# Channel mixing in six blocks of 512 tokens, some across two batches, in place of eight blocks of 384

## The chip, the cores and the metric

The kernel runs on one core of one Trainium2 chip. The metric is the device time of one execution in microseconds (us), and the median over the runs is compared. The core has a matrix engine (PE, with its weight loads listed apart as PEld), a vector engine (DVE), a scalar engine (ACT), GpSimd (POOL) and a queue engine (SP) that issues most of the transfers. Matmul results land in PSUM, in which this kernel keeps eight buffers, called banks here: four under the tag `sc` (among them `po`), three under `sh` (`ph`, `yp`) and one under `xT`.

## What is computed

A decayed causal attention over 4 batches, 8 heads, 768 tokens and head size 64 gives `x` of shape (4, 768, 512). A mixer follows: first over the tokens of each batch, then over the channels of each token.

```python
def _moe_ref(x, w_tok1, w_tok2, w_ch1, w_ch2):
    xt = x.transpose(0, 2, 1)
    h = np.maximum(xt @ w_tok1, 0.0) @ w_tok2
    u = x + h.transpose(0, 2, 1)
    h2 = np.maximum(u @ w_ch1, 0.0) @ w_ch2
    return (u + h2).astype(np.float32)
```

The change concerns the last three lines, the channel mixing: `u` is 4 x 768 = 3072 tokens of 512 channels, `w_ch1` is 512 x 1536 and `w_ch2` is 1536 x 512. Each token is independent of the others there, so the 3072 tokens can be cut into blocks anywhere.

## The kernel before

The activations lie in SBUF transposed, with the channels on the partitions: `uT[b]` is a tile of 128 partitions x 4 channel groups x 768 tokens for each batch `b`. Attention writes it (L299), the token mixing adds to it (L441), the channel mixing reads it and adds to it again (L629).

To keep float32 accuracy, each operand of a mixing matmul is split into a high and a low part in a 32-bit matmul type, and each product is three matmuls: high x high, low x high, high x low. The token mixing does that at L416 (256 columns) and L436 (384 columns).

The channel mixing takes the tokens in eight blocks (b, sh), half a batch of `SB` = 384 tokens each, and the 1536 hidden channels in six groups of 256 (`NG` = 6, two tiles of 128, `jj`, in each). A unit is one pair (group g, block k); the 48 units go group by group. In a unit:

- `mm1(g, k, jj)` for the two `jj`: 12 matmuls of 128 x 384 into one PSUM bank `ph` (4 channel groups x 3 products, L605), then ACT makes the high part of the ReLU, `hh` (L609), and DVE the low part, `hl` (L610).
- `mm2` of the unit before, one for each of the four output channel groups t: 6 matmuls into a bank `po` (L626) and one DVE addition into `uT` (L629). So each unit has 24 matmuls of `mm1` and 24 of `mm2`, all of 384 columns; mm1 of this unit and mm2 of the one before alternate: mm1, two mm2, mm1, two mm2.

The high and low parts of a block's tokens, `uh` and `ul`, are made once by `split_block`: four steps, each an ACT cast (L500) and a POOL subtraction (L501). Blocks 0 and 1 are split during attention, put on a list of small steps, `waiting`, that is worked off between the other instructions; the others are split in the units of the first group, one block ahead.

The weights of a group arrive as 64-bit words by DMA and are narrowed in four pieces by a chain of one ACT, five DVE, one ACT and one POOL instruction of 512 elements (L342 to L360). Each piece is loaded in one unit of the group before and worked off through `waiting` in the next.

The last ten pieces of the token mixing (the list `groups`, of which attention takes 38 of 48) are spread over the first units by `rest`: two in unit 0, four in unit 1, four in unit 2. In the last group the finished blocks 0 to 6 are turned by DVE (L636) into a buffer `y`, of which there are two, and written to memory by 16 DMAs per block from SP (L641). The last block is turned by PE (L650) into bank `yp`, copied by ACT (L654) into `ylast`, and written by three DMAs (L658): one for t = 0 and 1 from ACT, one for t = 2 from SP, one for t = 3 from ACT.

The order of all engines is the order in which the code is written (a manual schedule); each engine runs its instructions in that order, except that PE's weight loads run ahead.

Of the kernel before, what the change touches and what calls it, by code (L numbers as in the profile page):

```python
# [9 lines left out]
F32 = mybir.dt.float32  # L10
F32R = mybir.dt.float32r
# [10 lines left out]
def kernel(  # L22
# [35 lines left out]


    ET = mybir.EngineType  # L60
# [2 lines left out]
    waiting = deque()  # L63
# [5 lines left out]


    upool = ctx.enter_context(tc.tile_pool(name="upool", bufs=1))
    uT = [upool.tile([P, NP, S], F32, name=f"uT{b}") for b in range(B)]
    ident = upool.tile([P, P], F32, name="ident")
    wa = ctx.enter_context(tc.tile_pool(name="wa", bufs=1))
    up = ctx.enter_context(tc.tile_pool(name="up", bufs=1))
# [3 lines left out]
    def bank(tag, nm, n):  # L79
        return ps.tile([P, n], F32, tag=tag, bufs={"sc": 4, "xT": 1, "sh": 3}[tag], name=nm)  # L80
# [82 lines left out]
    n = 1  # L163
# [282 lines left out]
    NG = NJ // JG  # L446
# [38 lines left out]
        return w[:, i * 1024 : (i + 1) * 1024], w[:, 2048:2560], w[:, 2560:3072]  # L485


    blocks = [(b, sh) for b in range(B) for sh in range(2)]
    uhl = {}

    def split_block(k, pool):

        b, sh = blocks[k]
        ub = uT[b][:, :, sh * SB : (sh + 1) * SB]
        uh = pool.tile([P, 4, SB], F32R, name=f"uh{k}")
        ul = pool.tile([P, 4, SB], F32R, name=f"ul{k}")
        uhl[k] = uh, ul

        def step(t):
            nc.scalar.copy(out=uh[:, t], in_=ub[:, t])  # L500
            nc.gpsimd.tensor_sub(out=ul[:, t], in0=ub[:, t], in1=uh[:, t].bitcast(F32))  # L501

        return [lambda t=t: step(t) for t in range(4)]

# [17 lines left out]
    for i in range(-2, NI):  # L522
        if 0 <= i + 1 < NI:
            scores(i + 1)
            scale_q(i + 1)
        if i >= 0:
            outputs(i, 0)
        place = state(i + 1) if 0 <= i + 1 < NI else None
        if i >= 0:
            outputs(i, 1)  # L530
        if i + 2 < NI:
            turn_q(i + 2)
        work = [groups.popleft() for _ in range(take.get(i, 0))]
# [24 lines left out]
        if i + 4 < NI:  # L558
            load_kq(i + 4)
        if i == -1:  # L560
            load_w1()
        if i == 1:
            load_w2()
        if 0 <= i < 3:
            convert_w1(i)
        if 2 <= i < 4:
            convert_w2(i - 2)
        if i == 3:
            convert_w2(2)
        if i == 5:  # L570
            weights[0], load, convert = load_group(0, wa, early_scratch)
        if 5 <= i < 9:
            load(i - 5)
        if 6 <= i < 10:
            convert(i - 6)
        if i == 9:
            waiting.extend(split_block(0, up))
        if i == 11:
            waiting.extend(split_block(1, up))
    later(99)  # L580
    att.close()
    wp = ctx.enter_context(tc.tile_pool(name="wp", bufs=1, reuse_waits="tile"))
# [2 lines left out]
    cp = None  # L585
# [10 lines left out]
    def mm1(g, k, jj):  # L596
        uh, ul = uhl[k]
        c1h, c1l, _, _ = weights[g]
        js = slice(jj * P, (jj + 1) * P)
        nm = f"{g}{k}{jj}"  # L600
        ph = bank("sh", f"ph2{nm}", SB)
        i = 0
        for ct in range(4):
            for w, x in ((c1h, uh), (c1l, uh), (c1h, ul)):
                nc.tensor.matmul(out=ph, lhsT=w[:, ct, js], rhs=x[:, ct], start=(i == 0), stop=(i == 11))  # L605
                i += 1
        hh = hp.tile([P, SB], F32R, tag="hh2", name=f"hh2{nm}")
        hl = hp.tile([P, SB], F32R, tag="hl2", name=f"hl2{nm}")
        nc.scalar.activation(hh, ph, AF.Relu)  # L609
        nc.vector.scalar_tensor_tensor(  # L610
            out=hl, in0=ph, scalar=0.0, in1=hh.bitcast(F32), op0=ALU.max, op1=ALU.subtract
        )
        hs[g, k, jj] = (hh, hl)

    ys = {}

    def mm2(g, k, t):
        b, sh = blocks[k]
        _, _, c2h, c2l = weights[g]
        po = bank("sc", f"po{g}{k}{t}", SB)  # L620
        cs = slice(t * P, (t + 1) * P)
        i = 0
        for jj in range(JG):
            hh, hl = hs[g, k, jj]
            for w, h in ((c2h, hh), (c2l, hh), (c2h, hl)):
                nc.tensor.matmul(out=po, lhsT=w[:, jj, cs], rhs=h, start=(i == 0), stop=(i == 3 * JG - 1))  # L626
                i += 1
        ub = uT[b][:, t, sh * SB : (sh + 1) * SB]
        nc.vector.tensor_add(out=ub, in0=po, in1=ub)  # L629
        if g < NG - 1 or k == len(blocks) - 1:  # L630
            return

        if t == 0:
            ys[k] = cp.tile([P, SB // 32, 4, 32], F32, tag="y", bufs=2, name=f"y{k}")
        y = ys[k]
        nc.vector.transpose(out=y[:, :, t, :], in_=ub)  # L636
        if t % 2 == 1:
            to = out[b, sh * SB : (sh + 1) * SB].rearrange("(blk s) (t q c) -> q s blk t c", s=32, t=4, q=4)
            for n in range(4):
                for tt in (t - 1, t):  # L640
                    nc.sync.dma_start(out=to[n, :, :, tt], in_=y[n * 32 : (n + 1) * 32, :, tt])  # L641

    def finish(t, ylast):

        k = len(blocks) - 1
        b, sh = blocks[k]
        yp = bank("sh", f"yp{t}", SB)
        for c in range(SB // P):
            cs = slice(c * P, (c + 1) * P)
            nc.tensor.transpose(  # L650
                out=yp[:, cs], in_=uT[b][:, t, sh * SB + c * P : sh * SB + (c + 1) * P], identity=ident
            )
        es = slice(t * P, (t + 1) * P)
        nc.scalar.copy(out=ylast[:, :, es], in_=yp.rearrange("p (c e) -> p c e", e=P))  # L654
        to = out[b, sh * SB : (sh + 1) * SB].rearrange("(c s) e -> s c e", s=P)
        if t > 0:
            es = slice(0 if t == 1 else t * P, (t + 1) * P)
            (nc.sync if t == 2 else nc.scalar).dma_start(out=to[:, :, es], in_=ylast[:, :, es])  # L658

    units = [(g, k) for g in range(NG) for k in range(len(blocks))]  # L660
    rest = [[], [], []]
    for n, g in enumerate(groups):
        rest[0 if n < 2 else 1 + (n - 2) // 4].append(g)
    splits = deque()
    for i, (g, k) in enumerate(units):
        if i == 3:
            p1.close()
            cp = ctx.enter_context(tc.tile_pool(name="cp", bufs=1, side="right", reuse_waits="tile"))
        if g == 0 and 2 <= k + 1 < len(blocks):
            splits.extend(split_block(k + 1, uq if k < 3 else cp))  # L670
        first = 1 if g == 0 else 0
        if g + 1 < NG:
            if k == first:
                weights[g + 1], load, convert = load_group(g + 1, wa if g % 2 else wp, scratch)
            if first <= k < first + 4:
                load(k - first)
            if first < k < first + 5:
                convert(k - first - 1)
        for x in range(2):
            for jj in range(x * JG // 2, (x + 1) * JG // 2):  # L680
                mm1(g, k, jj)
                later(2)
            for _ in range(4):
                if splits:
                    splits.popleft()()
            for t in (2 * x, 2 * x + 1):
                if i < len(rest) and t < len(rest[i]):
                    rest[i][t]()
                if i >= 1:
                    mm2(*units[i - 1], t)  # L690
                    later(1)
    ylast = cp.tile([P, SB // P, DM], F32, name="ylast")
    for t in range(4):
        mm2(*units[-1], t)
        if t >= 2:
# [30 lines left out]
```

## Time and profile before

| What | Value |
|---|---|
| device time, median of 3 runs | 612.38 us (612.28 to 614.78) |
| span of the profiled execution, first to last instruction | 1471.3 us |
| PE busy in it | 1461.3 us of the span, 4426 matmuls |
| channel mixing, matmuls | 1152 at L605 and 1152 at L626, 384 columns each |
| first matmul after the start of the span | 5.65 us |
| last matmul of the channel mixing to the end of the span | 6.8 us |
| DVE, ACT, POOL busy in it | 343.6, 154.9, 159.2 us |

The profiled execution is a different one from the timed runs, and it is 2.4 times as long as their median; no device time beside its span is recorded for it. Matmuls overlap in the trace (one starts before the listed end of the one before), so what a matmul costs is read from the distance of starts, or from the chain of work that ended last, and not from the mean duration of one. A row of a group of instructions reads: line, engine, operation, output<-inputs, shape, count | busy us, mean ns of one | idle us of the engine just before them and who ended the idle time.

### The profile page before, as it was taken

To read this page: it belongs to the slowest core of one execution; us is meant where nothing else is said; L and a number is where in the kernel's file an instruction comes from. 1 tells how busy PE (TensorE), PEld (TensorE's weight loads), DVE (VectorE), ACT (ScalarE), POOL (GpSimd) and SP (SyncE) were. 2 spreads that over 40 slices of the span, in tenths; PEclk is the share of its full clock that TensorE was granted. 3 is DMA by queue.
4 is the path that set the end of the run, shared out by engine and by line. 5 is a ranking of instruction groups with operands and counts; after the bars stand their busy time and mean duration, and the time that the engine had idled before them with its cause. 6 is when DMAs were issued, how large, how long until landed. Compare 5 with 4: busy or idle time off the path is not lost.

```text
span 1471.3 us, 10762 instructions
## 1 busy us (share of the span) xinstructions
PE 1461.3 (99%) x4426; PEld 1160.3 (79%) x4426; DVE 343.6 (23%) x654; ACT 154.9 (11%) x315; POOL 159.2 (11%) x155
## 2 busy tenths in 40 slices
PE   8999999999999999999999999999999999999998
PEld 6788788798887777777777777777777777777776
DVE  3333233312111222122211221122211222112222
ACT  2221111110110111000000110010000000000000
POOL 5242212231011121000000000000000000000000
DMA  9423331210000010001000000000000000002222
GB/s 193 108 44 68 71 69 33 43 33 15 15 1 14 15 29 0 0 29 29 0 1 14 29 14 0 0 24 20 15 0 0 29 0 0 0 11 40 36 35 51
DMA packets 144498, 41.61 MB, mean 28 GB/s; under 512 B 137664, under 2 KB 138816, under 8 KB 144448
## 3 DMA queue, kind: packets, MB, share of 16 engines
q1 hardware_dynamic: 143504, 40.32, 13.2%
q8 instruction: 35, 0.57, 0.2%
q10 hardware_dynamic: 944, 0.59, 0.1%
q14 instruction: 15, 0.12, 0.0%
HBM read 34.61 MB, written 6.29 MB: 28 GB/s over the span
## 4 chain that ended last, share of the span: by engine, by line
PE 99%; DMA 0%; ACT 0%; SPq 0%; issue 0%
PE po L626 35%; PE ph L605 35%; PE ph L416 6%; PE pu L436 6%; PE sc L258 4%; PE xT L282 4%; PE xT L292 3%; PE kt L183 2%; PE xp L314 2%; PE kv L225 2%; PE qt L200 1%; DMA kn<-in_k_dram 0%; PE yp L650 0%; ACT uT L299 0%; ACT ylast L654 0%; SPq L100 0%
## 5 line engine op out<-in xcount | busy, mean ns | idle before, releaser
L605 PE MATMUL ph<-uh,c1h 128*128 128x384 f32 x384 | 261.2, 680 | 0.0
L605 PE MATMUL ph<-uh,c1l 128*128 128x384 f32 x384 | 261.1, 680 | 0.0
L626 PE MATMUL po<-hl,c2h 128*128 128x384 f32 x384 | 260.9, 679 | 0.0
L626 PE MATMUL po<-hh,c2h 128*128 128x384 f32 x384 | 260.6, 679 | 0.0
L605 PE MATMUL ph<-ul,c1h 128*128 128x384 f32 x384 | 260.5, 678 | 0.0
L626 PE MATMUL po<-hh,c2l 128*128 128x384 f32 x384 | 260.4, 678 | 0.0
L610 DVE SCALAR_TENSOR_TENSOR hl<-ph,hh 128x384 fp32r<-128x384 f32 x96 | 53.5, 557 | 657.9 <-ACT hh L609 617.6
L605 PEld LDWEIGHTS ph<-uh,c1l 128*128 128x128 f32 x384 | 136.1, 354 | 36.4 <-issue 32.3
L605 PEld LDWEIGHTS ph<-uh,c1h 128*128 128x128 f32 x384 | 135.3, 352 | 37.1 <-issue 33.2
L626 PEld LDWEIGHTS po<-hh,c2l 128*128 128x128 f32 x384 | 134.8, 351 | 37.5 <-issue 33.6
L626 PEld LDWEIGHTS po<-hh,c2h 128*128 128x128 f32 x384 | 134.8, 351 | 37.3 <-issue 29.0
L626 PEld LDWEIGHTS po<-hl,c2h 128*128 128x128 f32 x384 | 134.7, 351 | 37.3 <-issue 31.4
L605 PEld LDWEIGHTS ph<-ul,c1h 128*128 128x128 f32 x384 | 135.2, 352 | 36.4 <-issue 32.4
L609 ACT ACTIVATE hh<-ph 128x384 fp32r<-128x384 f32 x96 | 47.1, 491 | 923.8 <-PE po L626 648.7
L629 DVE TENSOR_TENSOR uT<-po,uT 128x384 f32<-128x384 f32 x192 | 104.5, 553 | 165.1 <-PE po L626 163.5
L282 PE MATMUL xT<-a,vn 128*64 128x128 f32 x384 | 75.0, 515 | 0.6 <-ACT uT L299 0.6
L343 POOL TENSOR_TENSOR c1l<-wa,c1h 128x512 fp32r<-128x512 f32 x10 | 12.7, 1272 | 509.0 <-ACT c1h L342 509.0
L292 PE MATMUL xT<-qs,stb 128*64 128x128 f32 x320 | 67.8, 541 | 0.0
L258 PEld LDWEIGHTS sc<-qT,kT 64*128 64x128 f32 x384 | 55.3, 425 | 8.6 <-issue 7.6
L258 PE MATMUL sc<-qT,kT 64*128 64x128 f32 x384 | 61.9, 535 | 0.0
L416 PE MATMUL ph<-xhi,w1h 128*128 128x256 f32 x96 | 53.9, 561 | 0.0
L416 PE MATMUL ph<-xhi,w1l 128*128 128x256 f32 x96 | 50.9, 530 | 0.0
(77 smaller groups left out, 1091.6 us busy)
## 6 DMA issues: line engine op xcount, KB each, us to landing
raw<-in_moe_w_ch_dram SPq DMA_DIRECT2D x20, 512.0 KB, 3.6
kn<-in_k_dram SPq DMA_DIRECT2D x32, 192.0 KB, 3.3
vn<-in_v_dram SPq DMA_DIRECT2D x16, 384.0 KB, 3.6
out_dram<-y SPq DMA_DIRECT2D x112, 48.0 KB, 1.8
qn<-in_q_dram SPq DMA_DIRECT2D x44, 96.0 KB, 3.6
uT<-in_moe_w_tok_dram SPq DMA_DIRECT2D x2, 1536.0 KB, 8.0
uT<-in_moe_w_ch_dram SPq DMA_DIRECT2D x4, 512.0 KB, 3.9
qn<-in_q_dram SPq DMA_DIRECT2D x10, 192.0 KB, 4.5
```

Source lines behind the costliest of these rows:

```text
L183: nc.tensor.transpose(out=kt[:, c * P : (c + 1) * P], in_=kn[:, 3 * g + c].rearrange("p h d -> p (h d)"), identity=ident,)
L225: nc.tensor.matmul(out=to[h * D : (h + 1) * D, c, :], lhsT=kds[i][:, h, c, :], rhs=vns[i][:, h, c, :], start=(c == 0), stop=(c == NC - 2),)
L258: nc.tensor.matmul(out=sc[h][:, c * P : (c + 1) * P], lhsT=kTs[i][r, cs], rhs=qTs[i][r, cs], start=True, stop=True,)
L282: nc.tensor.matmul(out=xT[h * D : (h + 1) * D, cs], lhsT=vns[i][:, h, c, :], rhs=weights_of[i, g, h][:, cg, :], start=(cg == 0), stop=False,)
L292: nc.tensor.matmul(out=xT[h * D : (h + 1) * D, cs], lhsT=st[:, c - 1, h, :], rhs=qss[i][:, c - 1, :], start=False, stop=(cg == 2),)
L416: nc.tensor.matmul(out=ph, lhsT=w[:, c, fs], rhs=x[:, c], start=(i == 0), stop=(i == 3 * NC - 1))
L436: nc.tensor.matmul(out=pu, lhsT=h[:, kk, cs], rhs=w[:, kk, ss], start=(i == 0), stop=(i == 3 * NK - 1))
L605: nc.tensor.matmul(out=ph, lhsT=w[:, ct, js], rhs=x[:, ct], start=(i == 0), stop=(i == 11))
L609: nc.scalar.activation(hh, ph, AF.Relu)
L610: nc.vector.scalar_tensor_tensor(out=hl, in0=ph, scalar=0.0, in1=hh.bitcast(F32), op0=ALU.max, op1=ALU.subtract)
L626: nc.tensor.matmul(out=po, lhsT=w[:, jj, cs], rhs=h, start=(i == 0), stop=(i == 3 * JG - 1))
L629: nc.vector.tensor_add(out=ub, in0=po, in1=ub)
```

## The change

The channel mixing takes the 3072 tokens in `NB` = 6 blocks of `CB` = 512. 512 is two thirds of 768, so of three blocks two lie in one batch each and the middle one takes the last third of one batch and the first third of the next. To address both with one pattern, the four tiles `uT[b]` become one tile `U` of 128 x 48 x 256: batch, channel group and third of the batch in the middle dimension. `block(k, t)` gives the two thirds of block k for channel group t, as a 128 x 2 x 256 pattern.

```diff
+    CB = 512
+    NB = B * S // CB
-    uT = [upool.tile([P, NP, S], F32, name=f"uT{b}") for b in range(B)]
+    U = upool.tile([P, B * NP * 3, S // 3], F32, name="uT")
+    uT = [U[:, b * NP * 3 : (b + 1) * NP * 3].rearrange("p (t c) s -> p t (c s)", t=NP) for b in range(B)]
...
-    blocks = [(b, sh) for b in range(B) for sh in range(2)]
+    def block(k, t):
+        (b, c), (b1, c1) = divmod(2 * k, 3), divmod(2 * k + 1, 3)
+        i, j = 3 * (b * NP + t) + c, 3 * (b1 * NP + t) + c1
+        return U[:, i : j + 1 : j - i]
+    def two(x):
+        return x.rearrange("p (n s) -> p n s", n=2)
...
-            nc.scalar.copy(out=uh[:, t], in_=ub[:, t])
-            nc.gpsimd.tensor_sub(out=ul[:, t], in0=ub[:, t], in1=uh[:, t].bitcast(F32))
+            ub = block(k, t)
+            nc.scalar.copy(out=two(uh[:, t]), in_=ub)
+            nc.gpsimd.tensor_sub(out=two(ul[:, t]), in0=ub, in1=two(uh[:, t]).bitcast(F32))
...
-        if i == 11:
-            waiting.extend(split_block(1, up))
...
-        ph = bank("sh", f"ph2{nm}", SB)
+        ph = bank("sh", f"ph2{nm}", CB)
...
-        po = bank("sc", f"po{g}{k}{t}", SB)
+        po = bank("sc", f"po{g}{k}{t}", CB)
...
-        ub = uT[b][:, t, sh * SB : (sh + 1) * SB]
-        nc.vector.tensor_add(out=ub, in0=po, in1=ub)
+        ub = block(k, t)
+        nc.vector.tensor_add(out=ub, in0=two(po), in1=ub)
...
-    rest = [[], [], []]
+    rest = [[[], [], [], []] for _ in range(2)]
     for n, g in enumerate(groups):
-        rest[0 if n < 2 else 1 + (n - 2) // 4].append(g)
+        i, t = (0, n) if n < 4 else (1, (n - 4) * 2 // 3)
+        rest[i][t].append(g)
...
-        if i == 3:
+        if i == 2:
             p1.close()
...
-        if g == 0 and 2 <= k + 1 < len(blocks):
-            splits.extend(split_block(k + 1, uq if k < 3 else cp))
+        if g == 0 and k + 1 < NB:
+            splits.extend(split_block(k + 1, uq if k < 2 else cp))
...
-    ylast = cp.tile([P, SB // P, DM], F32, name="ylast")
+    ylast = cp.tile([P, CB // 32, 4, 32], F32, tag="y", bufs=2, name="ylast")
+    ylast = ylast.rearrange("p a b c -> p (a b c)").rearrange("p (c e) -> p c e", e=DM)
```

The buffers `uh`, `ul`, `hh`, `hl`, `y` and `ylast` grow with the block, `ylast` now takes one of the two `y` buffers, the writes to memory follow the new blocks, and in a unit the pieces of `rest` now come after `mm2` and not before it. There are 36 units in place of 48, and 1728 matmuls of 512 columns in place of 2304 of 384 in the channel mixing.

The first place is PE where unit 0 ends and unit 1 begins (names end in group, block and `jj`: `ph2001` is group 0, block 0, second `jj`; `ph2010` is block 1; `pu` is token mixing). Before:

```order
L605 MATMUL ph2001_2523<-uh0_1667,c1l0_1038 128x384
L605 MATMUL ph2001_2523<-ul0_1668,c1h0_1037 128x384
L605 MATMUL ph2010_2550<-uh1_1981,c1h0_1037 128x384
L605 MATMUL ph2010_2550<-uh1_1981,c1l0_1038 128x384
L605 MATMUL ph2010_2550<-ul1_1982,c1h0_1037 128x384
```

And in the changed kernel:

```order
L439 MATMUL pu310_2545<-w2h_124,hl3_2360 128x384
L439 MATMUL pu310_2545<-w2l_125,hh3_2359 128x384
L613 MATMUL ph2010_2563<-uh1_2451,c1h0_1034 128x512
L613 MATMUL ph2010_2563<-uh1_2451,c1l0_1035 128x512
L613 MATMUL ph2010_2563<-ul1_2452,c1h0_1034 128x512
```

Two pieces of the token mixing (`pu300` and `pu310`, twelve matmuls) now stand between the second mm1 of unit 0 and the first mm1 of unit 1; the matmuls themselves are 512 wide.

The second place is ACT from the last attention cast into unit 1 (`uh1` and `uh2` are the high parts of blocks 1 and 2, `hh3` belongs to the token mixing of batch 3, `hh2...` to the channel mixing). Before:

```order
L420 ACTIVATE hh3_2372<-ph301_2433 128x256
L609 ACTIVATE hh2000_2477<-ph2000_2464 128x384
L420 ACTIVATE hh3_2372<-ph310_2481 128x256
L420 ACTIVATE hh3_2372<-ph311_2502 128x256
L609 ACTIVATE hh2001_2536<-ph2001_2523 128x384
L609 ACTIVATE hh2010_2563<-ph2010_2550 128x384
L500 CAST uh2_2540<-uT1_61 128x384 x4
```

And in the changed kernel:

```order
L423 ACTIVATE hh3_2359<-ph301_2420 128x256
L617 ACTIVATE hh2000_2466<-ph2000_2453 128x512
L510 CAST uh1_2451<-uT_60 128x512 x4
L423 ACTIVATE hh3_2359<-ph310_2478 128x256
L423 ACTIVATE hh3_2359<-ph311_2499 128x256
L617 ACTIVATE hh2001_2533<-ph2001_2520 128x512
L617 ACTIVATE hh2010_2576<-ph2010_2563 128x512
L510 CAST uh2_2553<-uT_60 128x512 x4
```

The four casts of block 1 have left the attention loop and stand in unit 0 behind its first ReLU; POOL's four subtractions for `ul1` moved with them.

The third place is the end of PE's work (`po573` and `po553` are the last output group of the last unit, `yp` the turned last block). Before:

```order
L626 MATMUL po573_6207<-hh2571_6147,c2l5_4925 128x384
L626 MATMUL po573_6207<-hl2571_6148,c2h5_4924 128x384
L650 MATMUL yp1_6215<-ident_64,uT3_63 128x128 x3
L650 MATMUL yp2_6221<-ident_64,uT3_63 128x128 x3
L650 MATMUL yp3_6227<-ident_64,uT3_63 128x128 x3
```

And in the changed kernel:

```order
L634 MATMUL po553_5351<-hh2551_5290,c2l5_4374 128x512
L634 MATMUL po553_5351<-hl2551_5291,c2h5_4373 128x512
L657 MATMUL yp1_5359<-ident_61,uT_60 128x128 x4
L657 MATMUL yp2_5366<-ident_61,uT_60 128x128 x4
L657 MATMUL yp3_5373<-ident_61,uT_60 128x128 x4
```

Twelve turns in place of nine stand behind the last matmul of the channel mixing.

More of the change, by code (lines that the diff above doesn't have):

```diff
@@ L485, in early_scratch @@
         return w[:, i * 1024 : (i + 1) * 1024], w[:, 2048:2560], w[:, 2560:3072]
-    blocks = [(b, sh) for b in range(B) for sh in range(2)]
+    def block(k, t):
[4 more added lines that the diff above has]
+        return x.rearrange("p (n s) -> p n s", n=2)
     uhl = {}
     def split_block(k, pool):
[L493 to L496, printed above, removed]
+        uh = pool.tile([P, 4, CB], F32R, name=f"uh{k}")
+        ul = pool.tile([P, 4, CB], F32R, name=f"ul{k}")
         uhl[k] = uh, ul
         def step(t):
-            nc.scalar.copy(out=uh[:, t], in_=ub[:, t])
-            nc.gpsimd.tensor_sub(out=ul[:, t], in0=ub[:, t], in1=uh[:, t].bitcast(F32))
+            ub = block(k, t)
+            nc.scalar.copy(out=two(uh[:, t]), in_=ub)
+            nc.gpsimd.tensor_sub(out=two(ul[:, t]), in0=ub, in1=two(uh[:, t]).bitcast(F32))
         return [lambda t=t: step(t) for t in range(4)]
@@ L606, in mm1 @@
                 i += 1
-        hh = hp.tile([P, SB], F32R, tag="hh2", name=f"hh2{nm}")
-        hl = hp.tile([P, SB], F32R, tag="hl2", name=f"hl2{nm}")
+        hh = hp.tile([P, CB], F32R, tag="hh2", name=f"hh2{nm}")
+        hl = hp.tile([P, CB], F32R, tag="hl2", name=f"hl2{nm}")
         nc.scalar.activation(hh, ph, AF.Relu)
@@ L615 @@
     ys = {}
+    rows = out.rearrange("b s e -> (b s) e")
     def mm2(g, k, t):
-        b, sh = blocks[k]
         _, _, c2h, c2l = weights[g]
-        po = bank("sc", f"po{g}{k}{t}", SB)
+        po = bank("sc", f"po{g}{k}{t}", CB)
         cs = slice(t * P, (t + 1) * P)
@@ L627, in mm2 @@
                 i += 1
-        ub = uT[b][:, t, sh * SB : (sh + 1) * SB]
-        nc.vector.tensor_add(out=ub, in0=po, in1=ub)
-        if g < NG - 1 or k == len(blocks) - 1:
+        ub = block(k, t)
+        nc.vector.tensor_add(out=ub, in0=two(po), in1=ub)
+        if g < NG - 1 or k == NB - 1:
             return
         if t == 0:
-            ys[k] = cp.tile([P, SB // 32, 4, 32], F32, tag="y", bufs=2, name=f"y{k}")
+            ys[k] = cp.tile([P, CB // 32, 4, 32], F32, tag="y", bufs=2, name=f"y{k}")
         y = ys[k]
@@ L637, in mm2 @@
         if t % 2 == 1:
-            to = out[b, sh * SB : (sh + 1) * SB].rearrange("(blk s) (t q c) -> q s blk t c", s=32, t=4, q=4)
+            to = rows[k * CB : (k + 1) * CB].rearrange("(blk s) (t q c) -> q s blk t c", s=32, t=4, q=4)
             for n in range(4):
@@ L643, in finish @@
     def finish(t, ylast):
[L645 to L648, printed above, removed]
+        k = NB - 1
+        yp = bank("sh", f"yp{t}", CB)
+        for c in range(CB // P):
             cs = slice(c * P, (c + 1) * P)
-            nc.tensor.transpose(
-                out=yp[:, cs], in_=uT[b][:, t, sh * SB + c * P : sh * SB + (c + 1) * P], identity=ident
-            )
+            nc.tensor.transpose(out=yp[:, cs], in_=uT[B - 1][:, t, S - CB + c * P : S - CB + (c + 1) * P], identity=ident)
         es = slice(t * P, (t + 1) * P)
         nc.scalar.copy(out=ylast[:, :, es], in_=yp.rearrange("p (c e) -> p c e", e=P))
-        to = out[b, sh * SB : (sh + 1) * SB].rearrange("(c s) e -> s c e", s=P)
+        to = rows[k * CB : (k + 1) * CB].rearrange("(c s) e -> s c e", s=P)
         if t > 0:
@@ L658, in finish @@
             (nc.sync if t == 2 else nc.scalar).dma_start(out=to[:, :, es], in_=ylast[:, :, es])
-    units = [(g, k) for g in range(NG) for k in range(len(blocks))]
-    rest = [[], [], []]
+    units = [(g, k) for g in range(NG) for k in range(NB)]
+    rest = [[[], [], [], []] for _ in range(2)]
     for n, g in enumerate(groups):
-        rest[0 if n < 2 else 1 + (n - 2) // 4].append(g)
+        i, t = (0, n) if n < 4 else (1, (n - 4) * 2 // 3)
+        rest[i][t].append(g)
     splits = deque()
     for i, (g, k) in enumerate(units):
-        if i == 3:
+        if i == 2:
             p1.close()
             cp = ctx.enter_context(tc.tile_pool(name="cp", bufs=1, side="right", reuse_waits="tile"))
-        if g == 0 and 2 <= k + 1 < len(blocks):
-            splits.extend(split_block(k + 1, uq if k < 3 else cp))
+        if g == 0 and k + 1 < NB:
+            splits.extend(split_block(k + 1, uq if k < 2 else cp))
         first = 1 if g == 0 else 0
@@ L691 @@
                     later(1)
-    ylast = cp.tile([P, SB // P, DM], F32, name="ylast")
+                if i < len(rest):
+                    for f in rest[i][t]:
+                        f()
+    ylast = cp.tile([P, CB // 32, 4, 32], F32, tag="y", bufs=2, name="ylast")
+    ylast = ylast.rearrange("p a b c -> p (a b c)").rearrange("p (c e) -> p c e", e=DM)
     for t in range(4):
```

2 lines of the change are left out of this document (removed).

## The prediction

> **What bounds the kernel now.** I read the clock first, then the page's head, then the chain of work that ended last, then PE's waits.
>
> ```profile
> core 0: 1471.3 us, clock 1.000
> span 1471.3 us, 10762 instructions
> PE 1461.3 (99%) x4426; PEld 1160.3 (79%) x4426; DVE 343.6 (23%) x654; ACT 154.9 (11%) x315; POOL 159.2 (11%) x155
> by line: PE po L626 35.0%; PE ph L605 35.0%; PE ph L416 5.8%; PE pu L436 5.8%; PE sc L258 4.1%; PE xT L282 4.0%; PE xT L292 3.2%; PE kt L183 2.0%; PE xp L314 1.9%; PE kv L225 1.6%; PE qt L200 0.6%; DMA kn<-in_k_dram 0.3%; PE yp L650 0.2%; A
> PE kt L183 <- DMA kn<-in_k_dram: 5.6, 1, 5.6
> PE xT L282 <- ACT uT L299: 0.6, 1, 0.6
> ```
>
> PE is the bound: the chain runs through PE from the first transfer to the end, and PE waits 5.6 us for that transfer, 0.6 us once more, and never again. 70% of the chain is the 2304 matmuls that the change rewrites.
>
> The profiled execution is 2.4 times as long as the median, 612.38 us. With PE busy throughout in the profile, the timed runs can only be shorter if PE itself runs faster there. So durations of PE rows must be scaled; those of ACT, DVE, POOL and DMA I take as they stand. Taking away the first wait (5.65 us) and the end behind the last channel matmul (6.8 us, rows below), the pace is (612.38 - 12.45) / (1471.3 - 12.45) = 0.411.
>
> **Fewer, wider matmuls.** Columns stay the same: 2304 x 384 = 1728 x 512 = 884,736. So only what a matmul costs beside its columns can be saved. The chain prices two widths. At 384 columns: 70.0% of 1471.3 us is 1029.9 us, over 2304 matmuls 447.0 ns each. At 256 columns (L416, 288 matmuls): 5.8% is 85.3 us, 296.3 ns each. That is 1.164 and 1.157 ns per column. A line through both has a constant of 3 x 296.3 - 2 x 447.0 = -5 ns; a share is rounded to 0.05%, 0.74 us, which moves 296.3 by 2.6 ns and the constant to anything from -14 to +4 ns. So the row says: proportional to the columns, and a constant of at most 4 ns. Scaled, 512 columns cost 447.0 x 4/3 x 0.411 = 245 ns against 184 ns now.
>
> 576 matmuls fewer save 576 x 4 ns = 2.3 us at the top and cost 576 x 14 ns x 0.411 = 3.3 us at the bottom. I take 2.4 ns, **-1.4 us**: an instruction less is no loss by itself, so the upper half is nearer.
>
> A rule of the Trainium skill ("TensorE: Matmul & The Clock Gate", section "Back-to-back issue gap") gives another size: for streams of weight load and matmul it states a sustained 81 ns at 128 columns and 131 ns at 512. A line through these has a constant of 64 ns, and by it the change would save 576 x 64 ns, 37 us. At 256 and 384 columns it would make 97 to 114 ns, a ratio of 1.17; the chain's ratio here is 447.0 / 296.3 = 1.51, so the trace disagrees.
>
> **What waits on the wider tiles.** ACT and DVE work per matmul result grows with the width, PE's time for it too:
>
> ```profile
> L610 DVE SCALAR_TENSOR_TENSOR hl<-ph,hh 128x384 fp32r<-128x384 f32 x96 | 53.5, 557 | 657.9 <-ACT hh L609 617.6 <-PE po L626 40.3
> L609 ACT ACTIVATE hh<-ph 128x384 fp32r<-128x384 f32 x96 | 47.1, 491 | 923.8 <-PE po L626 648.7 <-PE ph L605 275.0
> L421 DVE SCALAR_TENSOR_TENSOR hl<-ph,hh 128x256 fp32r<-128x256 f32 x16 | 6.8, 424 | 85.5 <-ACT hh L420 85.5
> L420 ACT ACTIVATE hh<-ph 128x256 fp32r<-128x256 f32 x16 | 6.1, 383 | 74.4 <-PE ph L416 74.4
> L351 DVE SCALAR_TENSOR_TENSOR ws<-raw,ws 128x512 uint32<-128x512 uint32 x20 | 14.2, 711 | 0.0
> L360 DVE SCALAR_TENSOR_TENSOR wa<-wa,ws 128x512 uint32<-128x512 uint32 x20 | 13.8, 692 | 0.7
> L354 DVE TENSOR_SCALAR wa<-wa 128x512 f32<-128x512 f32 x20 | 8.3, 417 | 0.0
> ```
>
> 128 more columns add 133 ns on DVE and 108 ns on ACT. The tightest use is the last `hl` of a unit: between the mm1 that makes it and the mm2 that reads it PE has 24 other matmuls. Before that is 24 x 184 ns = 4.4 us at the timed pace, against 0.49 + 0.56 us plus a whole narrowing that DVE may have ahead of it (0.71 + 0.69 + three like L354, 0.42 us each = 2.7): 3.7 us. After: 5.9 us against 0.60 + 0.69 + 2.7 = 4.0 us. Covered before, more so after; nothing.
>
> **The split of block 1, moved into unit 0.** Its casts and subtractions now stand behind ACT's first ReLU. Rows of 512 columns on the same engines:
>
> ```profile
> L342 ACT CAST c1h<-wa 128x512 fp32r<-128x512 f32 x10 | 6.2, 620 | 16.9 <-DVE wa L360 16.9
> L343 POOL TENSOR_TENSOR c1l<-wa,c1h 128x512 fp32r<-128x512 f32 x10 | 12.7, 1272 | 509.0 <-ACT c1h L342 509.0
> ```
>
> From the end of unit 0's first mm1: 0.60 (ReLU) + 0.62 + 1.27 = 2.5 us to the first `ul1`, 2.5 + 3 x 1.27 = 6.3 us to the last. PE has until then two pieces of 18 matmuls of 256 columns (36 x 296.3 x 0.411 = 4.4 us), 12 of 512 (2.9 us) and the two moved pieces of the token mixing (12 x 184 ns = 2.2 us): 9.5 us. Covered by 3 us; nothing. The token mixing pieces keep their matmuls and only change places. The weights' narrowing has four units of a group of six; a unit is a third longer, so it is looser, too. One tile `U` for four adds no wait where the blocks don't overlap.
>
> **The writes of the last group.** SP issues 16 DMAs per block:
>
> ```profile
> L641 SPq DMA_DIRECT2D out_dram<-y x112: 315/467/1763, 1312.4 to 1457.8; - x112
> out_dram<-y SPq DMA_DIRECT2D x112, 48.0 KB, 1.8
> out_dram<-ylast ACTq DMA_DIRECT2D x1, 384.0 KB, 2.7
> out_dram<-ylast SPq DMA_DIRECT2D x1, 192.0 KB, 2.4
> out_dram<-ylast ACTq DMA_DIRECT2D x1, 192.0 KB, 2.1
> ```
>
> 16 x 0.467 = 7.5 us for a block whose unit takes PE 48 x 184 ns = 8.8 us at the timed pace: 85% full, so SP keeps up, but barely. If the mixing's share of the timed run is a tenth smaller, SP falls behind by some tenths of a us per block over seven blocks, and the DMA of t = 2 at the end comes up to about 1 us late. After: 80 issues, 7.5 us in 11.8 us, never behind, provided that an issue of 64 KB costs as one of 48 KB. Between 0 and -1 us: **-0.5 us**.
>
> **The end.** Behind the last channel matmul:
>
> ```profile
> 1464.09 0.72 PE L626 MATMUL po<-hl,c2h 128*128 128x384 f32 x1
> 1464.52 3.01 PE L650 MATMUL yp<-ident,uT 128*128 128x128 f32 x9
> 1464.85 0.56 DVE L629 TENSOR_TENSOR uT<-po,uT 128x384 f32<-128x384 f32 x1 [3.03 <-PE po L626]
> 1465.71 0.48 ACT L654 COPY ylast<-yp 128x384 f32<-128x384 f32 x1 [3.11 <-PE yp L650]
> 1467.57 0.48 ACT L654 COPY ylast<-yp 128x384 f32<-128x384 f32 x1 [0.43 <-PE yp L650]
> 1468.08 0.38 ACTq L658 DMA_DIRECT2D out_dram<-ylast  x1
> ```
>
> Twelve turns for nine: three more of 3.01 / 9 = 0.33 us, 1.0 us at the profile's pace, 0.41 us scaled. The last addition 0.13 us more, the last copy 0.11 us, the last DMA 256 KB for 192: from 2.1 or 2.4 us at 192 KB to 2.7 at 384, some 0.15 us. Sum 0.8 us, between 0.4 (turns hidden behind ACT) and 1.4 (turns at the profile's pace): **+0.8 us**.
>
> **Sum.** 612.38 - 1.4 - 0.5 + 0.8 = 611.3 us, 0.2% less. About 0.5%, 3.1 us, is what a measurement of this kernel can tell from no change, so I call this the same. In the profile, at its own pace, the sum is 1471.3 - 1.4 + 1.4: a span within 10 us of before.
>
> **Rivals.**
>
> *A constant that only the fast pace shows* (faster). Each matmul has one weight load of 128 columns, the same for 384 as for 512. At the profile's pace the loader has time:
>
> ```profile
> 901.44 0.24 PEld L626 LDWEIGHTS po<-hl,c2h 128*128 128x128 f32 x1 [0.18 <-issue]
> 901.87 0.45 PEld L626 LDWEIGHTS po<-hh,c2h 128*128 128x128 f32 x1 [0.19 <-ACT hh L609]
> ```
>
> 0.24 us, with 0.18 and 0.19 us idle before and after it. If loads, unlike matmuls, don't get faster by the whole 2.4, some ns per matmul may stick out at 184 ns. They can't be long: 0.24 us x 2304 = 553 us would leave 59 us for the rest, 30% of the chain. With 6 to 10 ns each the change saves 3.5 to 5.8 us: 609.2 to 606.9 with the end's +0.8 and the writes' -0.5. For it: nothing in the profile excludes it. Against: the chain at two widths has no such constant. 0.24.
>
> *A large constant* (faster). If a third of the 184 ns, 61 ns, were constant, 576 x 61 ns = 35.1 us would go: 577.5 us. Against: 256 columns would then cost 143 ns, 78% of 184, and the chain has 66%. 0.02. The figures of the Trainium skill quoted above come to nearly this.
>
> *Waits before the change that only the fast pace shows* (faster). The `hl` margin above is 0.7 us before and 1.9 after. Were PE late by 0.2 us in the 20 units with a narrowing, 4 us go: 607.3 us. 0.06.
>
> *PE takes steps in width* (slower). Starts of neighbours:
>
> ```profile
> 415.68 0.54 PE L416 MATMUL ph<-xlo,w1h 128*128 128x256 f32 x1
> 415.92 0.53 PE L416 MATMUL ph<-xhi,w1h 128*128 128x256 f32 x1
> 419.08 0.72 PE L605 MATMUL ph<-uh,c1l 128*128 128x384 f32 x1
> 419.51 0.72 PE L605 MATMUL ph<-ul,c1h 128*128 128x384 f32 x1
> ```
>
> 0.24 us at 256 columns, 0.43 at 384: undisturbed neighbours rise by 0.19 for 128 columns, more than in proportion. At that slope 512 columns take 0.62 us where 0.596 would be even: 1728 x 0.62 = 1071 us in place of 2304 x 0.433 = 998, 7% more. Scaled by 0.411: +30 us, 642 us. It decides as soon as the distance at 512 columns is over 4/3 of that at 384. Against: the means, which make the span, are in proportion. 0.06.
>
> *The split of block 1 comes late* (slower). If POOL or ACT is held up for over 3 us around unit 0, unit 1 waits once; all of its 5.1 us of subtractions exposed give 616.4 us. 0.05.
>
> **Chances.** The forecast, 0.57; faster by 0.24 + 0.02 + 0.06; slower 0.06 + 0.05. A little of the first rival's low end falls within 0.5%: faster 0.31, same 0.58, slower 0.11. The range goes from the first rival's far end with the writes' whole term, 606 us, to the bottom of the matmul term and the largest end, 612.38 + 3.3 + 1.4 = 617, cut to 616 since both ends at once are unlikely; it leaves out 577.5, 642 and part of the late split.
>
> **What would show it.** Right: the share of PE in the chain stays at 99%, both changed matmul lines have 1728 matmuls whose distance of starts averages 4/3 of 447 ns, PE's waits stay at the first transfer, and the end behind the last channel matmul grows from 6.8 us to about 8. Wrong: PE waiting in the first two units for `ul1`, a mean distance clearly off 596 ns, or a timed gain over 3 us with nothing waiting, which would make the constant of a matmul larger than 4 ns.

## The result, and the profile after

| | before | after |
|---|---|---|
| device time, median of four runs each | 613.58 us (612.28 to 614.94) | 604.81 us (600.82 to 606.61) |
| ratio, with 95% interval | | 0.9862 (0.9815 to 0.9908) |
| the same in another session (`after_again`) | 610.78 us | 603.14 us, ratio 0.9877 (0.9843 to 0.9911) |

The change makes the kernel faster by 7.6 to 8.8 us, 1.2 to 1.4%. The prediction said 611.3 us, no change, with a range down to 606: it was wrong, on the low side of its range.

The profile of before that the prediction quotes (1471.3 us) is 2.4 times as long as the timed runs, so the comparison below is with a second profile of the same kernel at the timed pace (`before_again`: span 610.7 us, device time of that execution 612.49). The profiled execution of after took 604.87 us, its span is 603.1 us. The granted clock is 0.993 in both.

The page of `before_again` has a row of the granted clock in 40 slices:

```profile
PEclk9989999999999999999999999999999999999998
```

The page of the 1471.3 us profile has no such row, and its trace holds no record of the clock. The 1.000 that the prediction quotes is what the view prints where nothing is recorded, not a measured clock.

The page of after, parts of its head, chain and main groups:

```profile
span 603.1 us, 9441 instructions
PE 581.8 (96%) x3854; PEld 493.9 (82%) x3854; DVE 327.0 (54%) x574; ACT 147.0 (24%) x283; POOL 162.0 (27%) x147
PE 89%; DVE 5%; DMA 2%; ACT 2%; issue 1%; SPq 0%; DVEq 0%; ACTq 0%
L618 DVE SCALAR_TENSOR_TENSOR hl<-ph,hh 128x512 fp32r<-128x512 f32 x72 | 49.8, 692 | 189.5 <-ACT hh L617 189.5
L617 ACT ACTIVATE hh<-ph 128x512 fp32r<-128x512 f32 x72 | 43.1, 599 | 288.8 <-PE po L634 221.4
```

PE is still the bound, but at the timed pace it is 89% of the chain (87% in `before_again`) and not 99%. Most of PE's waits lie in attention:

```profile
PE xT L285 <- ACT uT L302: 6.3, 4, 3.1
PE kt L186 <- DMA kn<-in_k_dram: 5.6, 1, 5.6
PE kv L228 <- POOL kd L210: 1.8, 2, 1.2
PE pu L439 <- DVE hl L618: 0.5, 1, 0.5
```

`before_again` has nearly the same first three, and then:

```profile
PE ph L605 <- DVE hl L610: 1.0, 2, 0.5
```

So in the mixing PE waits 1.0 us before and 0.5 us after. That half microsecond is a small part of the gain; the rest must be read from the matmuls themselves. A stretch of 280 us inside the mixing, in which PE does nothing but channel-mixing matmuls, as a row of the view by windows (from:to, length, PE busy and how many instructions, clock, DMA share, GB/s). `before_again`:

```profile
260.00:540.00 280.00, 280.00 (x1604) 1.00 0.09 27
```

And after:

```profile
260.00:540.00 280.00, 280.00 (x1223) 1.00 0.08 27
```

The row counts every matmul that reaches into the window, also those cut by its edges. So the distance from start to start is taken from the first and the last matmul counted. `before_again`:

```profile
259.83 0.34 PE L626 MATMUL po<-hh,c2h 128*128 128x384 f32 x1
539.84 0.33 PE L605 MATMUL ph<-uh,c1l 128*128 128x384 f32 x1
```

And after:

```profile
259.62 0.39 PE L613 MATMUL ph<-uh,c1h 128*128 128x512 f32 x1
539.80 0.39 PE L634 MATMUL po<-hh,c2l 128*128 128x512 f32 x1
```

That is 280.01 us / 1603 = 174.7 ns from start to start at 384 columns and 280.18 / 1222 = 229.3 ns at 512. In proportion to the columns 512 would take 232.9. The 3.6 ns that each wider matmul is under proportion make the first part of the gain: 2304 x 174.7 = 402.5 us, 1728 x 229.3 = 396.2 us, **6.3 us less**. First and last start of `mm1` and `mm2`, before:

```profile
L605 PE MATMUL ph<-uh,c1h x384: 334/337/443, 184.2 to 594.2; 128*128 128x384 f32 x192
L626 PE MATMUL po<-hl,c2h x384: 334/334/340, 196.2 to 601.4; 128*128 128x384 f32 x192
```

And after:

```profile
L613 PE MATMUL ph<-uh,c1h x288: 387/392/459, 185.2 to 586.6; 128*128 128x512 f32 x144
L634 PE MATMUL po<-hl,c2h x288: 387/389/397, 200.4 to 595.7; 128*128 128x512 f32 x144
```

From the first `mm1` to the last `mm2` it takes 601.4 - 184.2 = 417.2 us before, 595.7 - 185.2 = 410.5 after: 6.7 us less. This counts the waits too; the half microsecond that PE waits less is the likely rest.

The second part is the end. Before, from the last channel matmul:

```profile
601.37 0.34 PE L626 MATMUL po<-hl,c2h 128*128 128x384 f32 x1
601.55 1.42 PE L650 MATMUL yp<-ident,uT 128*128 128x128 f32 x9
603.24 0.40 ACTq L658 DMA_DIRECT2D out_dram<-ylast  x1
603.67 0.86 ACT L654 COPY ylast<-yp 128x384 f32<-128x384 f32 x2 [1.12 <-DMA out_dram<-y]
605.63 0.38 ACTq L658 DMA_DIRECT2D out_dram<-ylast  x1
606.95 0.58 SPq L658 DMA_DIRECT2D out_dram<-ylast  x1
```

And after:

```profile
595.70 0.40 PE L634 MATMUL po<-hl,c2h 128*128 128x512 f32 x1
595.93 1.67 PE L657 MATMUL yp<-ident,uT 128*128 128x128 f32 x12
597.19 0.40 ACTq L663 DMA_DIRECT2D out_dram<-ylast  x1
598.24 0.39 SPq L663 DMA_DIRECT2D out_dram<-ylast  x1
598.73 0.38 ACTq L663 DMA_DIRECT2D out_dram<-ylast  x1
```

The last DMA is issued 5.6 us after the last channel matmul before, and by SP, which was not free earlier; 3.0 us after it now, and by ACT. To the end of the span it takes 610.7 - 601.4 = 9.3 us before and 603.1 - 595.7 = 7.4 after, **1.9 us less**, although the tail itself has more to do. The third part is no effect of the change: the mixing starts at 184.2 us in the one execution and 185.2 in the other. In attention the granted clock falls for a few microseconds in some executions and not in others. The stretch from 30 to 50 us, with the clock as the third number from the right, in `before_again` and in after:

```profile
30.00:50.00 20.00, 15.36 (x210) 0.91 1.10 231
30.00:50.00 20.00, 15.42 (x195) 0.83 1.05 225
```

In `order_384`, `writes_act_384`, `loads_64` and `writes_half_512` the clock is 1.00 in this stretch and the mixing starts at 181.2 to 182.3 us; in `writes_half_384`, with 384 columns, it is 0.83 and the mixing starts at 185.0. So the start goes with the clock and not with the width. -6.7 - 1.9 + 1.0 = -7.6 us, the difference of the spans.

### The profile page after: what moved, and what is told of

Read it like the earlier page. It is cut to its first block, busy times and chain, and to the rows that moved or that the text cites. A ratio compares the mean times of both kernels' runs of the same rounds, so it can differ in the third digit from the quotient of the medians.

```text
span 603.1 us, 9441 instructions
## 1 busy us (share of the span) xinstructions
PE 581.8 (96%) x3854; PEld 493.9 (82%) x3854; DVE 327.0 (54%) x574; ACT 147.0 (24%) x283; POOL 162.0 (27%) x147
## 4 chain that ended last, share of the span: by engine, by line
PE 89%; DVE 5%; DMA 2%; ACT 2%; issue 1%; SPq 0%; DVEq 0%; ACTq 0%
PE ph L613 33%; PE po L634 33%; PE ph L419 6%; PE pu L439 5%; PE xT L285 3%; PE sc L261 3%; PE xT L295 2%; DMA uT<-in_moe_w_tok_dram 2%; PE kt L186 2%; PE kv L228 1%; PE xp L317 1%; DVE uT L354 1%; DMA qn<-in_q_dram 1%; DVE xlo L326 1%; DVE a L270 1%
## 5 line engine op out<-in xcount | busy, mean ns | idle before, releaser
L613 PE MATMUL ph<-ul,c1h 128*128 128x512 f32 x288 | 113.4, 394 | 0.0
L613 PE MATMUL ph<-uh,c1l 128*128 128x512 f32 x288 | 113.2, 393 | 0.0
L613 PE MATMUL ph<-uh,c1h 128*128 128x512 f32 x288 | 113.1, 393 | 0.0
L634 PE MATMUL po<-hh,c2l 128*128 128x512 f32 x288 | 112.8, 392 | 0.0
L634 PE MATMUL po<-hh,c2h 128*128 128x512 f32 x288 | 112.8, 392 | 0.0
L634 PE MATMUL po<-hl,c2h 128*128 128x512 f32 x288 | 112.0, 389 | 0.0
L637 DVE TENSOR_TENSOR uT<-po,uT 128x512 f32<-128x512 f32 x144 | 95.7, 683 | 8.3 <-PE po L634 8.0
L613 PEld LDWEIGHTS ph<-ul,c1h 128*128 128x128 f32 x288 | 54.1, 188 | 12.3
L613 PEld LDWEIGHTS ph<-uh,c1h 128*128 128x128 f32 x288 | 54.2, 188 | 12.1
L613 PEld LDWEIGHTS ph<-uh,c1l 128*128 128x128 f32 x288 | 54.0, 188 | 11.9
```

Of the source, the lines that this page charges most:

```text
L637: nc.vector.tensor_add(out=ub, in0=two(po), in1=ub)
```

## The experiments

Theory 1: a matmul has a constant that doesn't depend on its columns, and fewer matmuls save it. Theory 2: waits before the change that the change removes, by its order or its looser timing. Theory 3: SP's writes of `y` are late before, and hold up the end. All ratios are to the kernel before, on the same chip in the same session.

### The kernel before again

No edit. It gives a profile at the timed pace and the noise.

> The kernel before, unchanged, for a profile at the pace of the timed runs. Theory 1 (a constant per matmul): in the profile of the changed kernel neighbouring matmuls start 120 ns apart at 256 columns, 173 at 384 (token mixing) and 227 at 512, which is columns / 2.4 + 13 ns; so the channel mixing of before starts its matmuls 173 ns apart too, the two lines together take about 2304 x 0.175 = 403 us of the chain against 396 after, and PE waits no more in the channel mixing than after. Theory 2 (waits): the distance of starts is proportional to the columns or less, 170 ns, and PE shows waits for hl, hh or the weights of several us in the channel mixing. Theory 3 (the end): the span behind the last channel matmul is 2 us or more longer than the 7 us after, because the writes from SP come late. Time: 612 to 614 us by all.

610.65 us, ratio 0.9986 (0.9959 to 1.0013). Its rows stand above. In the 1471.3 us profile that the prediction quotes, a stretch of `mm1` and `mm2` alone reads:

```profile
600.00:1300.00 700.00, 700.00 (x1569) 1.00 0.04 11
```

700 us / 1569 = 446 ns (447 without the edges), where the other execution has 174.7 ns. The 1.00 in this row is no reading, as said above, so a lower clock of PE is not excluded; nor is it shown. ACT's ReLU at L609 takes 491 ns in the one and 492 in the other, so ACT kept its pace. Whatever slowed PE also hid the constant; how it did so stays open.

### Every channel matmul cut in two

The changed kernel, with each matmul of 512 columns done as two of 256, one half of the bank after the other: 3456 matmuls for 1728, everything else the same.

```diff
-        for ct in range(4):
-            for w, x in ((c1h, uh), (c1l, uh), (c1h, ul)):
-                nc.tensor.matmul(out=ph, lhsT=w[:, ct, js], rhs=x[:, ct], start=(i == 0), stop=(i == 11))
+        for n in range(2):
+            ns = slice(n * 256, (n + 1) * 256)
+            i = 0
...
+                    nc.tensor.matmul(
+                        out=ph[:, ns], lhsT=w[:, ct, js], rhs=x[:, ct, ns], start=(i == 0), stop=(i == 11)
+                    )
```

(and the same in `mm2`)

> The changed kernel with each matmul of the channel mixing cut into two of 256 columns, 3456 in place of 1728, same columns, same blocks, same other engines. Theory 1 (a constant of 13 ns per matmul): 1728 x 13 = 22.5 us slower than the changed kernel, about 627 us, starts 120 ns apart. Theory 2 or 3 (waits or the end): the number of matmuls matters by 4 ns each at most, up to 7 us slower, 605 to 612 us.

624.16 us, ratio 1.0205 (1.0171 to 1.0238), some 20 us above the changed kernel. The same window of its trace:

```profile
260.00:540.00 280.00, 280.00 (x2337) 1.00 0.09 28
```

Its first and last matmul counted:

```profile
259.77 0.28 PE L640 MATMUL po<-hh,c2l 128*128 128x256 f32 x1
539.92 0.28 PE L615 MATMUL ph<-uh,c1h 128*128 128x256 f32 x1
```

280.15 us / 2336 = 119.9 ns at 256 columns. A line through 256 and 512 has 0.427 ns per column and a constant of 2 x 119.93 - 229.28 = 10.6 ns; it gives 174.6 ns at 384, where 174.7 was measured. So three widths lie on one line with a constant of about 10.6 ns, and 1728 x 10.6 = 18.3 us is what the halves add (their span is 621.9, 18.8 us longer than after's). 576 x 10.6 = 6.1 us is what the change takes away by that line, 6.3 by the two measured distances. Theory 1 holds, in size too.

### Weights of 64 columns

If the constant were the weight load sticking out behind a matmul, a load of half the columns would shrink it. This kernel leaves out most products of the upper half of each result's outputs.

```diff
-                nc.tensor.matmul(out=ph, lhsT=w[:, ct, js], rhs=x[:, ct], start=(i == 0), stop=(i == 11))
+                m = P if i in (0, 11) else P // 2
+                nc.tensor.matmul(
+                    out=ph[:m], lhsT=w[:, ct, jj * P : jj * P + m], rhs=x[:, ct], start=(i == 0), stop=(i == 11)
+                )
```

(and in `mm2`, for the middle four of six)

> The changed kernel with 64 weight columns in place of 128 in ten of the twelve matmuls of each mm1 result and four of the six of each mm2 result (1296 of 1728); the first and last of each result keep 128, and the upper half of the outputs lacks the products left out. The matmuls stream the same 512 columns. Theory W (the constant of 11 to 13 ns is the change of weights and goes with their columns): half of it goes in 1296 matmuls, 7 to 8 us faster than the changed kernel. Theory I (a constant per instruction, whatever the weights): the same as the changed kernel within 1.5 us.

601.86 us, ratio 0.9863 (0.9832 to 0.9894): not to be told from the changed kernel in the same session (0.9877). Its loads and its window:

```profile
L614 PEld LDWEIGHTS ph<-uh,c1h 128*64 128x64 f32 (+1 forms) x288 | 42.4, 147 | 23.9
L614 PEld LDWEIGHTS ph<-uh,c1l 128*64 128x64 f32 x288 | 38.6, 134 | 23.8
```

```profile
260.00:540.00 280.00, 280.00 (x1219) 1.00 0.08 27
```

Where all loads of a group are of 64 columns they take 134 ns in place of 188 (`before_again` and after have 188), yet the distance of starts is 280.01 / 1218 = 229.9 ns (from 259.77 to 539.78 us), not less than the changed kernel's 229.3. At 512 columns the constant doesn't hang on how long the weight load takes. With 384 and 256 columns the shorter load was not tried; that one line fits all three widths speaks against a second cause there. What the constant is was not found.

### The moved order alone

The kernel before with 384 columns, but with the new places of the split of block 1 and of the token mixing's last pieces.

```diff
-        if i == 11:
-            waiting.extend(split_block(1, up))
...
+        i, t = (0, n) if n < 4 else (1, (n - 4) * 2 // 3)
+        rest[i][t].append(g)
...
-        if g == 0 and 2 <= k + 1 < len(blocks):
+        if g == 0 and k + 1 < len(blocks):
...
-                if i < len(rest) and t < len(rest[i]):
-                    rest[i][t]()
                 if i >= 1:
                     mm2(*units[i - 1], t)
                     later(1)
+                if i < len(rest):
+                    for f in rest[i][t]:
+                        f()
```

> Eight blocks of 384 as before, with the changed order alone: block 1 is split in unit 0 and not in attention, the ten left pieces of token mixing go four to unit 0 and six to unit 1, behind mm2. Theory 1 (a constant per matmul): no change, within 1.5 us of before. Rival (the moved steps): attention is relieved of four casts and four subtractions, and the gain of 8.8 us shows here in large part, 605 to 609 us.

611.44 us, ratio 0.9992 (0.9967 to 1.0016): by the timed runs the order is worth between -2.0 and +1.0 us. Its trace shows a little of Theory 2:

```profile
L603 PE MATMUL ph<-uh,c1h x384: 332/337/342, 182.2 to 591.4; 128*128 128x384 f32 x192
L624 PE MATMUL po<-hl,c2h x384: 334/334/338, 195.1 to 598.5; 128*128 128x384 f32 x192
PE pu L436 <- DVE hl L608: 0.5, 1, 0.5
```

From the first `mm1` to the last `mm2` it takes 598.5 - 182.2 = 416.3 us, 0.9 less than `before_again`, and PE waits for `hl` once for 0.5 us and not twice. So the order is worth up to 0.9 us of the 6.7, and the width the other 5.8 to 6.3.

### Half of the writes from another queue

To take the load from SP in the kernel before, the writes of every second `y` step were issued from ACT (`writes_act_384`) or from POOL (`writes_pool_384`).

```diff
-                    nc.sync.dma_start(out=to[n, :, :, tt], in_=y[n * 32 : (n + 1) * 32, :, tt])
+                    (nc.scalar if tt == t else nc.sync).dma_start(
+                        out=to[n, :, :, tt], in_=y[n * 32 : (n + 1) * 32, :, tt]
+                    )
```

> The kernel before with half of the y writes of the last group issued from ACT in place of SP, so that SP is half empty. Theory 3 (SP is full before the change and its last DMA comes late): 1 to 3 us faster than before. Theory 1: no change, within 1 us.

> The kernel before with half of the y writes of the last group issued from POOL, which does nothing else by then, so that SP is half empty and ACT is left alone. Theory 3 in its present form (SP is full from the first y write to the last, which costs the end of before about 2 us): 2 to 2.5 us faster than before, with 7 us or less from the last channel matmul to the end of the span in place of 9.3. Rival (the DMAs themselves, of 128 bytes a piece, are late, not SP): no change.

Both missed, on the slow side. From ACT: 624.01 us, ratio 1.0206 (1.0169 to 1.0242). From POOL (`nc.gpsimd` in place of `nc.scalar`): 623.3 us, ratio 1.0195 (1.0161 to 1.0228). ACT's waits in the first:

```profile
ACT hh L609 <- DMA out_dram<-y: 52.8, 11, 4.8
```

and PE's behind them:

```profile
PE po L626 <- ACT hh L609: 8.4, 4, 3.4
```

ACT makes the ReLUs that `mm2` needs. Its share of the writes stands between them in its order, so a write that isn't ready holds a ReLU, and the ReLU holds PE. POOL has no such work at the end, but issues more slowly:

```profile
585.11 1.23 POOL L641 DMA_DIRECT2D out_dram<-y  x2 [1.65 <-issue]
587.42 1.23 POOL L641 DMA_DIRECT2D out_dram<-y  x2 [1.07 <-issue]
589.70 1.25 POOL L641 DMA_DIRECT2D out_dram<-y  x2 [1.05 <-issue]
```

Two writes per 2.3 us, 1.15 us each, more than the 0.51 to 0.56 of SP (below): POOL falls behind in its turn, and its end comes 15.2 us after the last channel matmul. Both kernels replace SP's load by a worse one, so they say nothing on Theory 3.

### Half of the writes left out

The same question without another queue: of each pair of steps of `y` only the first is written, in the kernel before and in the changed one.

```diff
-                for tt in (t - 1, t):
+                for tt in (t - 1,):
```

> The kernel before without every second y write of the last group (56 of 112; the channel groups t = 1 and 3 of blocks 0 to 6 are not written), so that SP has half its work there and no other engine takes any. Theory 3 (SP, full from the first y write to the last, delays the end of before): 2 to 2.7 us faster than before, with 6.5 to 7.3 us from the last channel matmul to the end of the span in place of 9.3, and the same length of the channel mixing. Rival (SP's late writes are hidden behind the turns, copies and last DMAs): no change, within 0.7 us.

> The changed kernel without every second y write (40 of 80). Theory 3: SP keeps up after the change, so this gains nothing: the same as the changed kernel within 0.7 us, 7.4 us behind the last channel matmul. If it gains 2 us as well, the writes cost both kernels the same and are no part of the difference.

With 384 columns: 610.26 us, ratio 0.9969 (0.9949 to 0.9988), 0.7 to 3.1 us faster than before. With 512: 603.8 us, ratio 0.9881 (0.986 to 0.9903), the same as the changed kernel with all writes (0.9862 and 0.9877). The end of the first:

```profile
602.16 0.34 PE L626 MATMUL po<-hl,c2h 128*128 128x384 f32 x1
604.31 0.40 SPq L658 DMA_DIRECT2D out_dram<-ylast  x1
604.69 0.38 ACTq L658 DMA_DIRECT2D out_dram<-ylast  x1
```

SP issues its last DMA 2.1 us after the last channel matmul, where the full kernel does so after 5.6, and the span ends 608.4 - 602.2 = 6.2 us after it, not 9.3. The writes cost the kernel before up to 3.1 us, and the changed one nothing. Why they were late shows in SP's row of `before_again`:

```profile
559.94 46.90 SPq L641 DMA_DIRECT2D out_dram<-y  x84
```

and of after:

```profile
559.88 37.03 SPq L649 DMA_DIRECT2D out_dram<-y  x55
```

Before, 84 writes take 46.90 us, 0.56 us each on the average, and 16 of them 8.9 us; a unit of PE is 48 x 174.7 ns = 8.4 us. SP's last `y` write ends at 559.94 + 46.90 = 606.84 us, 5.5 us or ten writes behind the start of the last channel matmul. The average hides two paces, as two stretches of the same row and the group's durations (min/median/max in ns) show:

```profile
576.22 22.11 SPq L641 DMA_DIRECT2D out_dram<-y  x43
597.87 8.97 SPq L641 DMA_DIRECT2D out_dram<-y  x14
L641 SPq DMA_DIRECT2D out_dram<-y x112: 316/468/2004, 542.6 to 606.4; - x112
```

In the first stretch a write costs 0.514 us and 16 cost 8.2 us, 98% of a unit. In the last it is 0.64 us, and single issues take up to 2.0 us; what they wait for the profile doesn't say. SP has no slack to make such delays up. After, a unit is 48 x 229.3 ns = 11.0 us, and 55 writes in 37.03 us come 0.67 us apart, 16 in 10.8 us: SP keeps step with the units, although single issues take up to 1.9 us there too.

Leaving writes out lightens the DMA engines as well as SP. That SP's order is what holds up the end is read from the rows: its last DMA follows 0.1 us behind its last `y` write, and a `y` write lands 1.9 us after its issue before and 2.0 us after.

### A wider token mixing on top

If 10.6 ns per matmul go, the token mixing's 288 matmuls of 256 columns (L419) could become 144 of 512: 144 x 10.6 = 1.5 us. The changed kernel, with `token_hidden` on all 512 channels at once; the pieces then come later in attention, and its inputs `xhi` and `xlo` have one buffer of full width in place of two of half.

```diff
-    def token_hidden(b, half, kk):
+    def token_hidden(b, kk):
...
-        ph = bank("sh", f"ph{b}{half}{kk}", DM // 2)
+        ph = bank("sh", f"ph{b}{kk}", DM)
...
-        for half in range(2):
-            for f in range(NK):
-                groups.append(lambda b=b, half=half, f=f: token_hidden(b, half, f))
+        for f in range(NK):
+            groups.append(lambda b=b, f=f: token_hidden(b, f))
...
-    take = {4: 2, 5: 2, 6: 5, 7: 4, 8: 2, 9: 4, 10: 5, 11: 2, 12: 2, 13: 5, 14: 4, 15: 1}
-    early = {4: 2, 8: 1}
+    take = {4: 2, 6: 4, 7: 4, 8: 2, 9: 3, 10: 3, 11: 2, 12: 2, 13: 3, 14: 3, 15: 2}
+    early = {4: 2, 8: 2, 12: 2}
```

> The changed kernel with the first token mixing product 512 columns wide too (L416 of before: 144 matmuls of 512 in place of 288 of 256), each batch's pieces a little later in attention. Theory 1 (a constant of 11 to 13 ns per matmul): 144 x 12 = 1.7 us faster than the changed kernel. Rival: in attention PE waits for others anyway, and the two pieces now stand together ahead of the next batch, 0 to 3 us slower.

606.9 us, ratio 0.9933 (0.9907 to 0.996), 3.8 us slower than the changed kernel. Its waits of PE:

```profile
PE xT L285 <- ACT uT L302: 7.4, 6, 2.7
PE xp L314 <- DVE xlo L323: 2.1, 1, 2.1
PE pu L433 <- DVE uT L438: 1.2, 2, 1.0
```

The last two are not among the waits of after: with the larger pieces PE meets DVE's results too early; whether the single buffer has a part in it was not tried. And the stretch from the first `mm1` to the last `mm2` is 414.4 us, not 410.5: the two pieces left for the first units now have 36 matmuls of 512 columns and not of 256, 36 x (229.3 - 119.9) = 3.9 us. Attention lost that work and did not get shorter (the mixing starts at 184.4 us, in `after_again` at 184.8). So attention is not bound by PE alone, and in this schedule the constant saved there bought nothing.

### The changed kernel again

> The changed kernel once more, beside the others on one chip. By all theories 0.985 to 0.990 of before.

603.14 us, ratio 0.9877 (0.9843 to 0.9911), span 602.7 us: 410.5 us of mixing and 7.4 us of end, as in the first profile of after. No kernel of this study is faster than the change and writes the whole output.

## Why the prediction was wrong, step by step

**PE is the bound.** Right in the mixing, which is what the change touches. The 99% was true of the 1471.3 us profile alone; at the timed pace it is 87% before and 89% after.

**Fewer, wider matmuls: -1.4 us.** This step failed. Its words were "proportional to the columns, and a constant of at most 4 ns". At the timed pace the constant is 10.6 ns, and the term is -6.1 to -6.3 us (-6.7 with the wait that went). The chain's shares were read correctly, 447.0 ns against 447 in the window, but from an execution in which 256 columns took 2.47 times and 384 columns 2.56 times what they take at the timed pace (296.3 / 119.9 and 447.0 / 174.7): one factor for all of PE was the error. It also mis-sized the distances, 184 and 245 ns for 174.7 and 229.3. The prediction's own sign came: a gain of over 3 us with little waiting, which it said would make the constant larger than 4 ns.

The rule of the Trainium skill ("TensorE: Matmul & The Clock Gate", "Back-to-back issue gap") was rightly not followed: its sustained 131 ns at 512 columns stands against 229.3 here, and the constant of 64 ns worked out from it against 10.6. The same section's other formula, for an isolated matmul at the warm clock, columns / 2.4 + 2.5 ns, is nearer: as an estimate it gives 215.8 ns at 512 and 162.5 at 384, where 229.3 and 174.7 were measured, with nearly the right slope (0.417 ns per column, here 0.427) and too small a constant.

**The first rival,** a constant that only the fast pace shows, named the right effect and nearly the right price, 6 to 10 ns. Its cause, a weight load that sticks out, is refuted at 512 columns by `loads_64`.

**What waits on the wider tiles, the split, the order: nothing.** Right for the time after the change: ACT takes 599 ns and DVE 692 per result, as estimated (0.60 and 0.69), and PE waits only 0.5 us in the mixing. But before the change PE waited 1.0 us, so the rival of waits that only the fast pace shows held in small: up to 0.9 us by the stretch of `order_384`, where it named 4, and at another place: PE waited with an `mm1`, which does not read `hl` itself.

**The writes of the last group: -0.5 us.** The mechanism was right, the size wrong: -3.1 us by the ends of the profiles, 0.7 to 3.1 by the timed runs. The step took an issue's own duration, 0.467 us, and a unit of 8.8 us, 85% full. Undisturbed issues come 0.514 us apart and the unit is 8.4 us, 98% full; with the long issues it is 0.56 us, 106%. The prediction's own line showed a longest issue of 1763 ns, which the sum left out.

**The end: +0.8 us.** Right within its bounds: 6.2 us without the writes' delay before, 7.4 after (with half of its writes left out also 7.4), +1.2. As a whole the end got shorter, 9.3 to 7.4 us, where the prediction expected it to grow, because of the writes.

**The sum.** -6.7 - 3.1 + 1.2 = -8.6 us, against -7.6 to -8.8 measured. The bottom of the range was the first rival's far end, 10 ns per matmul, with 1 us for the writes: 612.38 - 5.8 - 1.0 + 0.8 = 606.4. The matmuls came out little beyond that, and the writes' delay by three times as much. The forecast itself missed because the matmul term's bounds, 2.3 us down and 3.3 up, came from the rounding of a share in one execution, not from the doubt whether that execution could show a constant.

## What to carry to other kernels

Where the profiled execution runs at another pace than the timed ones, its ratios between shapes are in doubt as well as its durations; take a profile at the timed pace before a constant per instruction is excluded, and see whether the page has a row of the clock at all. A queue's price per transfer is the distance of starts in a stretch where it has no pause, and the longest issue belongs beside the median: here a queue that was 85% full by durations was at 98% by distances and had nothing left for the long ones. On a stream of matmuls that PE runs without a gap, price the number of instructions as well as the columns: here 0.427 ns per column and 10.6 ns per matmul.

## What the runs showed of the hardware that was not expected

- The distance of starts of these 32-bit matmuls lies on a line at 256, 384 and 512 columns: 119.9, 174.7 and 229.3 ns. At 512 columns, weights of 64 columns in place of 128 don't shorten it (229.9), though the load takes 134 ns and not 188.
- One program was profiled at two paces, 447 and 174.7 ns per matmul of 384 columns. The slow execution left no record of the clock. What sets PE's pace there stays open; no run here tried it.
- The granted clock fell to 0.91 or 0.83 in the mean of 30 to 50 us in some executions and stayed at 1.00 in others, with both kernels, and the mixing then started up to 4 us later.
- A write of 48 KB in pieces of 128 bytes costs SP 0.514 us from start to start in a stretch without long issues, 0.56 us on the average, and POOL 1.15 us; with half of the writes issued from ACT, the ReLUs waited behind them for 52.8 us in all, and PE for 8.4.
